# RWKV-6 and a hardswish MLP on one core: more fill products in the idle time of TensorE

## The chip, the cores and the metric

One of the eight cores of a Trainium2 chip runs the whole program. The metric is the device time of one execution in microseconds (us); "before" has a median of 565.46 us over five timed runs.

## The reference

An attention block in the manner of RWKV-6 on r, k, v, w of shape (4 batches, 8 heads, 768 steps, 48), float32, and then an MLP. The recurrence keeps a 48x48 state per batch and head:

```
for t in range(S):
    cur = u * k[t] (outer) v[t]
    y[t] = r[t] @ (state + cur)
    state = w[t][:, None] * state + k[t] (outer) v[t]
x = y transposed to (3072, 384)
h = x @ w_in                        # 384 x 2048
out = (h * clip(h + 3, 0, 6) / 6) @ w_out   # 2048 x 384
```

All products on TensorE are in float32. The weights arrive as 64-bit floats and are converted to float32 on the chip.

## The kernel before, in words

The 3072 tokens are 24 chunks of 128; four chunks make a block, so there are six blocks of the MLP. Per chunk the recurrence is done in closed form: two scans on VectorE give decays (L420, L429), r and k are scaled with them (L444, L440), TensorE makes the 64x64 scores (L488), transposes k (L504), makes the state product k'v (L588), reads the state (L566) and adds the scores' part (L575). The bonus u enters as a diagonal: r*k on VectorE (L453), a dot with u on TensorE (L463, called "the dot" below), a copy to ScalarE's side (L469), and eight scaled identities (L479) into the score tile, into which L495 copies the scores.

In block 0 the heads' last pair is read first (L566, L575), left by ScalarE (L630 or L632), spread with a selecting product (L640), then the rest is read (L566, L575) and left (L650, L652). As soon as chunks 0 and 1 are left, the first MLP products of block 0 follow: up (L695), clip on ScalarE (L685), gate on VectorE (L706). The weights' conversion goes on beside this: fetch (L379, by SP), ScalarE L388 and L392, VectorE L397, L402, L407. Three fetched tiles ("bits") at a time are held; the next fetch waits until L402 and L388 are done with an old one. L509 turns out the transposed k, L595 the state product, L517 and L533 update the state.

Nothing of the order is left to the hardware or a scheduler at run time: class `Plan` holds every step with its engine, an assumed duration, its predecessors, a due time and the buffers that it takes. `order()` plays the steps through with the assumed durations and gives one static order per engine; each engine then runs its list in order and waits at semaphores.

`emit()` writes the program out in that order. On the way it also writes fill products: `spin()` is a 128x128x128 float32 product of the identity with itself into a PSUM bank that is free at that time, and nobody reads it. Where the plan has TensorE idle between two steps, `int(FILL * hole / SPIN)` fill products go ahead of the second step; this lasts until the step "up0.0.0", the first up product of block 0, ahead of which none is put. `last` starts at `COLD` = 3.0, the planned time up to which the start is covered by four fill products that are written out by hand in `constants()`. The planned holes come from the assumed durations, not from the chip. A fill product stands in TensorE's queue as any other: what follows it on TensorE waits until it has been issued.

In the profile a float32 product shows as two records (a transpose as one).

## Time and profile before

| what | value |
|---|---|
| timed runs, five | median 565.46 us, 563.54 to 567.07 |
| profiled execution: time, span | 562.15 us, 560.2 us |
| TensorE (PE) busy | 541.9 us (97%) |
| VectorE (DVE) busy | 444.6 us (79%) |
| ScalarE (ACT) busy | 266.2 us (48%) |
| GpSimd (POOL) busy | 113.7 us (20%) |
| granted TensorE clock, mean | 0.986 |
| fill products (L1232), all before 23.6 us | 62 records, 31 products |
| first up product (L695) starts | 33.44 us |

The span runs from the first instruction to the last. PEclk in the strips is the clock granted to TensorE, in tenths of full speed; in tables of stretches it is a share. A name such as "PE ps L463" is engine, written tile, line. "idle before <- X" is the time in which the engine stood still ahead of an instruction, and what ended it.

### The profile page before, as it was taken

To read this page: it belongs to the slowest core of one execution; us is meant where nothing else is said; L and a number is where in the kernel's file an instruction comes from. 1 tells how busy PE (TensorE), PEld (TensorE's weight loads), DVE (VectorE), ACT (ScalarE), POOL (GpSimd) and SP (SyncE) were. 2 spreads that over 40 slices of the span, in tenths; PEclk is the share of its full clock that TensorE was granted. 3 is DMA by queue.
4 is the path that set the end of the run, shared out by engine and by line. 5 is a ranking of instruction groups with operands and counts; after the bars stand their busy time and mean duration, and the time that the engine had idled before them with its cause. 6 is when DMAs were issued, how large, how long until landed. Compare 5 with 4: busy or idle time off the path is not lost.

```text
span 560.2 us, 13278 instructions
## 1 busy us (share of the span) xinstructions
PE 541.9 (97%) x5512; PEld 482.7 (86%) x5512; DVE 444.6 (79%) x727; ACT 266.2 (48%) x657; POOL 113.7 (20%) x111
## 2 busy tenths in 40 slices
PE   7899999999899999999999999999999999999996
PEld 7788776778788899888899888899888899988995
DVE  6979999999979968789978789978797817087440
ACT  4677883653366524456524456524465720255100
POOL 2000000334263333145133144243321000000000
PEclk9879999999999999999999999999999999999999
DMA  8939823441342414765214765314500000100001
GB/s 258 277 125 330 279 96 102 133 139 29 115 153 81 102 56 157 237 193 156 95 57 157 235 197 151 100 56 157 185 16 0 10 8 15 43 1 1 1 15 48
DMA packets 23077, 63.96 MB, mean 114 GB/s; under 512 B 3120, under 2 KB 10352, under 8 KB 23008
## 3 DMA queue, kind: packets, MB, share of 16 engines
q1 hardware_dynamic: 22880, 63.02, 36.7%
q8 instruction: 45, 0.74, 0.6%
q14 instruction: 24, 0.20, 0.1%
q10 hardware_dynamic: 128, 0.00, 0.0%
HBM read 57.31 MB, written 4.72 MB: 111 GB/s over the span
## 4 chain that ended last, share of the span: by engine, by line
PE 66%; DVE 23%; DMA 4%; issue 2%; ACT 2%; SPq 1%; DVEq 0%; ACTq 0%
PE bank L866 24%; PE bank L809 23%; PE bankS L866 5%; PE bankS L809 4%; PE bank L695 3%; DMA bits<-in_moe_w_out_dram 2%; DVE E L420 2%; DVE g L826 2%; DVE W L429 2%; PE y_ps L566 1%; DMA xT<-xT 1%; PE y_ps L588 1%; PE ps L504 1%; PE bank L488 1%; DVE A L495 1%
## 5 line engine op out<-in xcount | busy, mean ns | idle before, releaser
L830 ACT ACTIVATE clip<-g,three 128x512 f32<-128x512 f32 x80 | 56.6, 719 | 43.6 <-DVE g L826 32.2
L826 DVE TENSOR_TENSOR g<-bank,g 128x512 f32<-128x512 f32 x80 | 53.7, 682 | 19.2 <-PE bank L809 19.0
L866 PE MATMUL bank<-w_out,g 128*128 128x192 f32 x352 | 63.3, 327 | 0.0
L834 DVE SCALAR_TENSOR_TENSOR g<-clip,g 128x512 f32<-128x512 f32 x80 | 57.8, 734 | 6.0 <-ACT clip L830 6.0
L866 PEld LDWEIGHTS bank<-w_out,g 128*128 128x128 f32 x352 | 58.0, 190 | 0.7
L440 POOL TENSOR_TENSOR K<-feat_in,E 112x512 f32<-112x512 f32 x17 | 21.9, 1290 | 152.1 <-DVE W L444 96.3
L479 ACT ACTIVATE A<-eyes,dg 128x64 f32<-128x64 f32 x192 | 49.0, 337 | 4.5 <-DVE dg L471 3.6
L882 ACT ACTIVATE o<-bank 128x192 f32<-128x192 f32 x33 | 10.9, 331 | 77.3 <-PE bank L866 77.3
L695 PE MATMUL bank<-xT,w_in 128*128 128x256 f32 x192 | 46.6, 393 | 1.0 <-DVE g L706 1.0
L695 PEld LDWEIGHTS bank<-xT,w_in 128*128 128x128 f32 x192 | 36.6, 196 | 7.4 <-DVE g L706 1.9
L662 ACT COPY xT<-y_ps 48x256 f32<-48x256 f32 x80 | 29.3, 366 | 28.8 <-PE y_ps L575 26.9
L809 PE MATMUL bank<-xT,w_in 128*128 128x256 f32 x160 | 41.4, 381 | 0.0
L824 ACT COPY g<-bank 128x512 f32<-128x512 f32 x50 | 28.9, 580 | 17.5 <-PE bank L809 17.3
L444 POOL TENSOR_TENSOR W<-feat_in,W 112x512 f32<-112x512 f32 x17 | 22.0, 1294 | 66.7 <-DVE W L429 66.7
L809 PEld LDWEIGHTS bank<-xT,w_in 128*128 128x128 f32 x160 | 29.9, 190 | 4.4 <-DVE g L826 0.4
L420 DVE TENSOR_TENSOR_SCAN E<-feat_in,back 112x520 f32<-112x520 f32 x24 | 30.4, 1269 | 2.7 <-POOL K L440 1.6
L809 PE MATMUL bank<-xT,bits 128*128 128x256 f32 x120 | 31.1, 381 | 0.0
L866 PE MATMUL bank<-more,g 128*128 128x192 f32 x176 | 30.5, 327 | 0.5 <-DVE o L884 0.5
L866 PE MATMUL bankS<-w_out,g 128*128 128x192 f32 x176 | 30.9, 327 | 0.0
L429 DVE TENSOR_TENSOR_SCAN W<-feat_in,start 112x520 f32<-112x520 f32 x24 | 29.8, 1245 | 1.1 <-PE y_ps L566 0.7
L866 PEld LDWEIGHTS bank<-more,g 128*128 128x128 f32 x176 | 28.6, 190 | 0.8 <-DVE o L884 0.8
L866 PEld LDWEIGHTS bankS<-w_out,g 128*128 128x128 f32 x176 | 28.7, 190 | 0.1
(285 smaller groups left out, 1160.7 us busy)
## 6 DMA issues: line engine op xcount, KB each, us to landing
feat_in<-in_feat_dram SPq DMA_DIRECT2D x23, 675.9 KB, 6.0
bits<-in_moe_w_in_dram SPq DMA_DIRECT2D x8, 768.0 KB, 9.1
bits<-in_moe_w_out_dram SPq DMA_DIRECT2D x8, 768.0 KB, 5.2
feat_in<-in_moe_w_in_dram SPq DMA_DIRECT2D x8, 768.0 KB, 4.4
feat_in<-in_moe_w_out_dram SPq DMA_DIRECT2D x8, 768.0 KB, 4.3
rk_in<-in_tok_dram SPq DMA_DIRECT2D x15, 384.0 KB, 6.0
v_in<-in_tok_dram SPq DMA_DIRECT2D x24, 192.0 KB, 4.2
out_dram<-o SPq DMA_DIRECT2D x24, 192.0 KB, 2.4
```

Source lines behind the costliest of these rows:

```text
L420: nc.vector.tensor_tensor_scan(out=E_[:, ::-1], data0=d["w"][:, :0:-1], data1=back.rearrange("q p t -> q (p t)")[:, ::-1], initial=0.0, op ...
L429: nc.vector.tensor_tensor_scan(out=W_, data0=d["w"][:, :-1], data1=starts[i % 2].rearrange("q p t -> q (p t)"), initial=0.0, op0=ALU.mult, ...
L444: early(i).tensor_mul(d["R"], d["r"], d["R"])
L479: nc.scalar.activation(out=d["A"][:, h, :], in_=eyes, func=ACT.Copy, scale=d["dg"][:, h])
L662: nc.scalar.copy(out=blocks[bk]["xT"][g * GP:g * GP + D, :, at:at + HL], in_=st[i]["y_ps"][a][(g ^ a) * GP:(g ^ a) * GP + D, :, :])
L695: nc.tensor.matmul(h_ps[:, :(c1 - c0) * L], lhsT=w_in[:, f // 2, j, f % 2, :], rhs=b["xT"][:, j, c0 * L:c1 * L], start=(j == 0), stop=(j = ...
L809: nc.tensor.matmul(b["p", d, c][:, z * HB:(z + 1) * HB], lhsT=weight(W_PLACE[r])[:, 2 * z + d, :], rhs=x_at(bk, X_PLACE[r]), start=fresh a ...
L824: nc.scalar.copy(out=out_, in_=src)
L826: nc.vector.tensor_tensor(out=out_, in0=src, in1=out_of(bk, d, other), op=ALU.add if sign > 0 else ALU.subtract)
L830: nc.scalar.activation(out=c, in_=out_of(bk, d, u), func=ACT.Relu, bias=three, scale=1.0)
L834: nc.vector.scalar_tensor_tensor(out=g, in0=blocks[bk]["r", d, u], scalar=6.0, in1=g, op0=ALU.min, op1=ALU.mult)
L866: nc.tensor.matmul(b["d", p, to][:, :h], lhsT=a, rhs=w(), start=(f == 0 and k in (1, 5)), stop=(f == HF - 1 and k in (2, 3, 4)), skip_grou ...
```

## The change

Two constants of the plan change. `FILL` goes from 0.75 to 1.0: a planned hole is filled wholly instead of three quarters. `SPIN`, the time that a fill product is reckoned to take, goes from 0.28 to 0.25 us: more of them are reckoned into the same hole. Both are used only in `emit()`, for the number of fill products; the plan's own order of steps does not depend on them.

```
-    SPIN = 0.28
-    FILL = 0.75
+    SPIN = 0.25
+    FILL = 1.0
     COLD = 3.0
     spin = until = None
```

## The prediction

> **What bounds the kernel now.** I read the strip of 40 slices first, for the TensorE clock.

> ```profile
> span 560.2 us, 13278 instructions
> ...
> PEclk9879999999999999999999999999999999999999
> ```

> The clock is below full only in the first three slices, 0 to 42 us, and that is where every fill product stands. The table of one-us stretches gives a clock of 0.96 in 15 to 16, 0.83 in 19 to 20, 0.58 in 26 to 27, 0.80 in 36 to 37, 0.50 between the first two and between the last two, and 1.00 elsewhere from 1 to 45. At half speed for the missing share, the clock fell at 15.92, rose at 19.33, fell at 26.16 and rose at 36.40. The distances are 3.41, 6.83 and 10.24 us: one, two and three steps of 3.41. So it is decided on a grid of that step, and I cut the table of stretches on the grid (columns: stretch, PE busy, PEld, DVE, ACT, POOL, clock, DMA share, GB/s).

> ```profile
> 9.09:12.51 3.42, 2.74 (x50) 2.56 (x51) 2.15 (x4) 2.12 (x10) 0.00 (x0) 1.00 1.05 360
> 12.51:15.92 3.41, 2.21 (x59) 1.77 (x49) 3.41 (x7) 2.90 (x11) 0.00 (x0) 1.00 1.08 373
> 15.92:19.33 3.41, 3.32 (x24) 2.74 (x24) 3.24 (x8) 3.34 (x6) 0.00 (x0) 0.50 1.05 210
> ...
> 22.75:26.16 3.41, 1.83 (x22) 1.37 (x22) 3.24 (x6) 1.96 (x8) 0.00 (x0) 1.00 1.02 292
> 26.16:29.57 3.41, 3.41 (x18) 3.41 (x18) 3.07 (x5) 2.19 (x10) 0.00 (x0) 0.50 1.05 382
> 29.57:32.99 3.42, 3.30 (x44) 2.83 (x44) 3.18 (x5) 1.84 (x5) 0.00 (x0) 0.50 0.36 130
> 32.99:36.40 3.41, 3.41 (x10) 2.87 (x11) 1.37 (x3) 2.23 (x11) 0.00 (x0) 0.50 0.00 0
> ...
> 67.12:70.53 3.41, 2.90 (x64) 2.41 (x62) 3.25 (x5) 2.89 (x4) 0.00 (x0) 1.00 0.99 339
> ```

> A stretch with PE busy 2.21 or 1.83 is followed by half clock; 2.74 and 2.90 keep it full. But 3.41 and 3.30 did not raise it again, and 3.32 did, so busy time is not the whole measure. I weigh each matmul record by its moving columns and by the share of the 128x128 array that it uses; transposes are left out. A fill record (128 columns, whole array) then counts 0.107 us. That gives 1.13 for the stretch at 9.09, 0.87 at 12.51, 0.65 at 22.75 and 0.98 at 67.12; at half clock, counted at full speed, 1.17 at 15.92 and 0.56 at 26.16. One mark between 0.87 and 0.98 explains all six. This measure is my inference.

> The chain of waits (start, us, what) shows what the second fall costs.

> ```profile
> 25.80 1.51 PE ps L463 x8
> 27.31 2.66 PE bank L640 x12
> 29.97 0.81 PE bank L566 x12
> ...
> 30.89 0.89 PE bank L575 x24
> 31.79 1.79 PE ps L463 x8
> 33.58 14.51 PE bank L695 x60
> ```

> From 25.80 on the chain is TensorE, nearly all of it at half clock. In the timeline VectorE pays for it (start, us, operation, idle before):

> ```profile
> 10.30 0.69 DVE L453 TENSOR_TENSOR rk<-feat_in 112x512 f32<-112x512 f32 x1 [2.03 <-DMA feat_in<-in_feat_dram]
> ...
> 33.80 0.56 DVE L397 TENSOR_SCALAR top<-bits 128x768 int32<-128x768 int32 x1
> 36.90 0.42 DVE L706 SCALAR_TENSOR_TENSOR g<-clip,bank 128x256 f32<-128x256 f32 x1 [2.54 <-ACT clip L685]
> ```

> It idles 2.54 us before the first gate (L706). The weight conversions stand behind that gate in its queue, SP's next fetch waits for the conversion L402 that ends at 38.18, and the DMA share is 0.00 from 33 to 39. So that idle time delays everything after it. The first fall costs nothing: from 10.30 to 25.6 VectorE has no wait over 0.14 us, and the chain lies on it.

> The fill products in the PE timeline, two records to a product:

> ```profile
> 1.43 5.63 PE L1232 MATMUL bankS<-ident 128*128 128x128 f32 x30 [1.43 <-POOL ident masks.py:199]
> ...
> 22.63 0.94 PE L1232 MATMUL bankS<-ident 128*128 128x128 f32 x6
> 24.71 0.32 PE L566 MATMUL bank<-W,S 48*48 48x64 f32 x4 [1.14 <-DVE S L517]
> ```

> **The change, part by part.** A planned hole of 1 us got 0.75/0.28 = 2.7 products and gets 1/0.25 = 4. In the built programs the holes go 15, 0, 4, 1, 4, 4, 3, 0 to 21, 1, 6, 2, 6, 6, 5, 1: 31 products to 48. Nothing else moves: the other engines' instructions and SP's queue keep their order. In the timeline 8 records started 0.11 us apart (the row of 1.07 us at 9.38, its last record 0.275 long), so a product takes 0.22 us at full clock; at half clock the 12 records of L640 in 2.80 us give 0.21 a record, 0.43 a product. So 17 x 0.22 = 3.8 us of TensorE work are added at full clock.

> *Before the first dot (+6).* The last 12 records run at full clock: +1.34 us. The fill now ends about 8.2, where L463 started at 7.12, so the first dot is 1.2 late. Behind it on PE wait the scores, the transposes, the second dot and the state product; on ACT, L469, the eight copies L479 (2.02) and L509. VectorE's next step waits for a DMA until 10.30 anyway, and the late dot has ended by 9.4. Followed along ACT: L469 at 9.3, copies to 11.6, L509 to 12.0; second dot 12.1 to 13.2, L469 13.2, copies 13.4 to 15.4, L509 to 15.8, L595 to 16.2. VectorE needs L595 at 16.55 (L517); before it ended at 15.92. Cost nothing; the cover left is 0.3 us.

> *The holes to 19.7 (+1, +2, +1, +2, +2).* The 1.2 us hole at 13.2 closes, since the second dot and the state product now fall into it, and the stretch at 12.51 gets several tenths more work: 0.87 rises well over 0.98. The clock should stay full at 15.92, so that six products take 1.3 us where four took 1.7. They end no later. Nothing won or lost: VectorE holds the chain.

> *The hole at 22.6 (+2).* Four more records lie ahead of a wait for VectorE (1.14 us, L517), so they cost nothing in time. They add 0.43 to the 0.65 of the stretch: 1.08, above the mark. By busy time alone it is 1.83 + 0.45 = 2.28, between 2.21 (fell) and 2.74 (kept). I take the first measure, since it alone also explains the rises.

> *Before L640 (+1).* This one lies on the path: 0.22 at full clock, 0.43 at half.

> **What it gives if the clock holds at 26.16.** From 25.80: dot 0.9, product 0.22 (the copies L630 end at 26.12, no wait), L640 1.34, L566 0.5, L575 with its drain and end 0.7, so about 29.5; the copies L650 and L652 take 0.97, during which the next dot runs; L695 from 30.6, its first six records 1.3 and an end of 0.16: 32.0, where it was 36.36. TensorE is 4.4 us earlier. VectorE cannot use all of that: its row L397 ends at 34.36, and of its own waits since 24.3 the 0.30 for L463 goes, so the gate comes at 34.0 for 36.90. ACT fits: copies to 33.4, clip (0.48) to 33.9. Gain 2.9. If the clock falls at 29.57 all the same, L695 ends its six records at 30.6 + 2.8 = 33.4, still ahead of VectorE, but the second gate, six records later at half clock, comes at about 36.5 for 38.28: gain 1.8. Late next are VectorE and the DMAs behind it, which keep the gain. I take 2.5. By the profiled execution's own time that is 562.15 - 2.5 = 559.65. That execution lay 3.3 under the median of the timed runs, 565.46; the difference is carried over: 565.46 - 2.5 = 563.0. Ends: 1.8 and the whole 4.4, so 561.1 to 563.7.

> [...]

> **Rivals.** *The clock falls at 26.16 all the same* (busy time decides; or the grid lies so that the thin stretch from 23.4 to 27.2 fills one step). Then TensorE is 0.43 later from L640 on, and the rise at 36.40 gives part back: +0.3, 565.8. For it: 2.28 is nearer to 2.21, and 0.8 us of idle remains. Against: the single mark.

> *The fill holds up the first dot for longer than its cover* (slower). The grid is tied to nothing in the trace that the kernel does, and the timed runs spread over 3.5 us. If the first rise came one step later, at 9.09, 42 records would end at about 9.9 and the first dot start 2.8 late; 30 end by 8.1, 1.0 late, which the cover takes. L595 would then end at about 17.95 and VectorE be 1.45 late; with 0.43 before L640 that is +1.9: 567.3. It decides once the first dot is later than about 8.5. Against: in this profile it is 8.2.

> *The change does nothing*: excluded for the counts, which differ; for the time it is the first rival.

> **How the numbers follow.** The clock holds: 0.55. It falls all the same: 0.27. The dot is late: 0.18. A measurement of this kernel tells 0.3% (1.7 us) from no change; the three lie at -2.5, +0.3 and +1.9, so faster 0.55, same 0.27, slower 0.18. The range reaches from the whole head start, 561.0, to the slower rival, 567.3; the likeliest case alone is 561.1 to 563.7.

> **What would show it.** Right: no half clock between 19 and 36 in the slices, L640 in about 1.45 us instead of 2.80, L695 starting near 31, the idle before the first L706 under 0.3 us, fetches starting again near 35, and L595 ending by 16.5. Wrong: L640 still 2.8 us long (first rival), or L517 after 16.9 with ACT named as what it waited for (slower rival).

## The result, and the profile after

The changed kernel takes as long as the one before: median 565.12 us (561.7 to 568.9, 52 runs) against 564.31 us (94 runs), ratio 1.0008, 95% interval 0.9996 to 1.0019. Ratios leave out single executions over 1.5% above the fastest of their kernel. The forecast was 563.0, reckoned from the 565.46 of five runs; from 564.31 the same gain would have been 561.8. The time lies in the range given, but that range spans the two rivals as well, and the case called likeliest did not occur: TensorE's clock still falls in the middle of block 0's first part. The profiled execution of after took 567.1 us, with a mean clock of 0.982.

The page of after, its span and the clock in 40 slices:

```profile
span 565.0 us, 13346 instructions
...
PEclk9979979999999999999999999999999999999999
```

The third slice (28 to 42 us) is below full as it was before, and slice 6 (70 to 85) is new. The second slice, low before, is full. Stretches of one us place the events: full from 5.93, half from 26.41 to 36.65 and from 70.79 to 77.61. The distances are again steps of 3.41 us. The table of stretches of after, cut on that grid (columns as in the prediction):

```profile
9.35:12.76 3.41, 3.41 (x56) 3.08 (x55) 2.77 (x4) 2.70 (x11) 0.00 (x0) 1.00 1.05 388
12.76:16.17 3.41, 3.41 (x83) 3.13 (x83) 3.41 (x8) 2.95 (x12) 0.00 (x0) 1.00 1.10 356
...
23.00:26.41 3.41, 2.26 (x28) 1.80 (x26) 3.27 (x5) 1.37 (x7) 0.00 (x0) 1.00 1.04 366
26.41:29.83 3.42, 3.42 (x23) 3.30 (x24) 3.28 (x6) 3.08 (x11) 0.00 (x0) 0.50 0.82 300
...
67.37:70.79 3.42, 2.90 (x66) 2.54 (x65) 3.39 (x5) 2.56 (x4) 0.00 (x0) 1.00 1.01 352
```

TensorE is busy without a gap from 9.35 to 16.17, and the fall that before had at 15.92 is gone. The stretch that ends at 26.41 holds 2.26 us of busy time where 2.28 was worked out, but by the prediction's weights its work is 0.66, where 1.08 was foreseen; before it was 0.65. The timeline of TensorE shows why (its first line is the first dot, 1.24 us later than before, where 1.2 was reckoned):

```profile
8.36 0.95 PE L463 MATMUL ps<-u_col,rk 112*128 112x2 f32 x8
...
22.29 1.38 PE L1232 MATMUL bankS<-ident 128*128 128x128 f32 x10
24.38 0.32 PE L566 MATMUL bank<-W,S 48*48 48x64 f32 x4 [0.71 <-DVE S L517]
...
26.88 2.66 PE L640 MATMUL bank<-xT,S__115 112*128 112x64 f32 x12
```

The ten fill records begin at 22.29, and the step that decides begins at 23.00: six of them start in the step ahead. What remains until 26.41 is small products, with few columns or little of the array in use. L640 takes 2.66 us, as before (2.80). VectorE, and the chain of waits of after (start, us, what), are therefore where they were:

```profile
36.47 0.42 DVE L706 SCALAR_TENSOR_TENSOR g<-clip,bank 128x256 f32<-128x256 f32 x1 [2.86 <-ACT clip L685]
```

```profile
25.47 1.02 PE ps L463 x8
26.49 0.59 PE bankS L1232 x2
27.09 2.45 PE bank L640 x12
```

The gate waits 2.86 us where it waited 2.54, and the added product before L640 is now a piece of the chain, 0.59 us at half clock, where 0.43 was reckoned. The fall at 70.79 holds up a gate as well; before has this gate at 75.80, without a wait:

```profile
77.50 0.42 DVE L706 SCALAR_TENSOR_TENSOR g<-clip,bank 128x256 f32<-128x256 f32 x1 [1.70 <-ACT clip L685]
```

### The profile page after: what moved, and what is told of

The parts are those of the page before. It is cut to its first block, busy times and chain, and to the rows that moved or that the text cites. A ratio compares the mean times of both kernels' runs of the same rounds, so it can differ in the third digit from the quotient of the medians.

```text
span 565.0 us, 13346 instructions
## 1 busy us (share of the span) xinstructions
PE 547.8 (97%) x5546; PEld 487.5 (86%) x5546; DVE 446.8 (79%) x727; ACT 265.9 (47%) x657; POOL 111.2 (20%) x111
## 4 chain that ended last, share of the span: by engine, by line
PE 68%; DVE 23%; DMA 3%; issue 2%; ACT 1%; SPq 0%; DVEq 0%
PE bank L866 24%; PE bank L809 21%; PE bank L695 6%; PE bankS L866 5%; PE bankS L809 4%; DVE g L826 2%; DMA xT<-xT 2%; DVE W L429 1%; DVE g L834 1%; DVE E L420 1%; DMA feat_in<-in_feat_dram 1%; PE y_ps L588 1%; PE y_ps L566 1%; DVE top L402 1%; DVE A L495 1%
## 5 line engine op out<-in xcount | busy, mean ns | idle before, releaser
L826 DVE TENSOR_TENSOR g<-bank,g 128x512 f32<-128x512 f32 x80 | 53.7, 682 | 18.1 <-PE bank L809 17.9
L479 ACT ACTIVATE A<-eyes,dg 128x64 f32<-128x64 f32 x192 | 49.0, 336 | 4.5 <-DVE dg L471 3.6
L695 PE MATMUL bank<-xT,w_in 128*128 128x256 f32 x192 | 48.5, 405 | 1.0 <-DVE g L706 1.0
L695 PEld LDWEIGHTS bank<-xT,w_in 128*128 128x128 f32 x192 | 38.2, 204 | 8.2 <-DVE g L706 1.7
L809 PE MATMUL bank<-xT,w_in 128*128 128x256 f32 x160 | 41.5, 382 | 0.6 <-DVE g L826 0.6
L809 PEld LDWEIGHTS bank<-xT,w_in 128*128 128x128 f32 x160 | 29.8, 190 | 5.5 <-DVE g L826 1.6
```

The lines of the kernel that those rows point to most:

```text
L479: nc.scalar.activation(out=d["A"][:, h, :], in_=eyes, func=ACT.Copy, scale=d["dg"][:, h])
L695: nc.tensor.matmul(h_ps[:, :(c1 - c0) * L], lhsT=w_in[:, f // 2, j, f % 2, :], rhs=b["xT"][:, j, c0 * L:c1 * L], start=(j == 0), stop=(j = ...
L809: nc.tensor.matmul(b["p", d, c][:, z * HB:(z + 1) * HB], lhsT=weight(W_PLACE[r])[:, 2 * z + d, :], rhs=x_at(bk, X_PLACE[r]), start=fresh a ...
L826: nc.vector.tensor_tensor(out=out_, in0=src, in1=out_of(bk, d, other), op=ALU.add if sign > 0 else ALU.subtract)
```

## The experiments

Two theories went in. *Theory one*: the clock falls between 22 and 31 us in nearly every execution, because the stretch with little weighted work is longer than one step; whatever the grid's phase, one whole step fits into it. I slid a window of 3.41 us over the trace: in before every window that starts from 22.4 to 31.8 weighs under 0.95, in after every one from 22.8 to 31.4; the thin stretch at 10 to 13 is gone in after. From 26 us on both traces run at half clock, which thins the windows by itself, so the slide alone does not show that the stretch would be as long at full clock. The profiles show that the fall is regular: all nine of kernels with fill of full width and without the nine products of held, below, have half clock somewhere between 22 and 36 us. *Theory two*: the clock is partly held, and the later first dot gives the gain back. Half-clock times below are 2 x span x (1 - mean clock), as the clock reads 1.00 or 0.50 in the profiles; they do not count the time before the first rise, where the tables have 1.00 though fill records start 0.21 us apart, for 0.11 behind it (before and after), and they count a fall at the very end (0.6 to 3.3 us in the profiles). By that every execution of after had 10.1 to 26.1 us of half clock, two steps or more, and 16.5 in the mean; where in an execution they lay, only its profile could tell.

Where no other edit is shown, a version only changes how many products stand ahead of a named step:

```
-    COLD = 3.0
+    COLD, MORE = 3.0, {...}
...
-   range(int(self.FILL * (self.start[n] - last) / self.SPIN) if n != self.until else 0)
+   range(int(self.FILL * (self.start[n] - last) / self.SPIN) + self.MORE.get(n, 0) if n != self.until else 0)
```

**held.** After, with `MORE = {'first1': 3, 'dot2': 2, 'read1': 1, 'dot3': 3}`: products through the whole thin stretch.

> The changed kernel with nine more fill products where the profile of after still shows thin work on TensorE: 3 before the first read of chunk 1 (8 instead of 5), 2 before the third dot (there were none), 1 before L640 (2 instead of 1), 3 before the fourth dot (there were none). Theory T1 (the clock falls between 22 and 27 us in nearly every execution, because the thin stretch is longer than one step of 3.41 and the change adds little in it): the clock now stays full from its first rise past 37 us, L640 takes about 1.45 us, the first gate L706 comes near 34 instead of 36.5, and the time falls by 2 to 3 us against before, 0.996. Theory T2 (the change holds the clock in part of the executions and the late first dot gives the gain back): half of that at most, about 1 us, since the dot is as late as in after.

Measured: 562.48 us median, ratio 0.9992 [0.9964, 1.002]; half clock 7.0 us in the mean. In its profile the clock is full from 5.92 to 558.9 us, L640 takes 1.45 us, and L695 starts at 31.45 (33.01 in after). So nine products in the right place hold the clock in this execution, and TensorE's price in the prediction (L640 in 1.45 us, L695 near 31) is met. Not in all: seven of the twelve executions have a mean clock of 0.994 or over and take 561.8 us in the mean, the other five, at 0.985 to 0.992, take 564.5. The gain over before can't be told from none here.

**narrow.** After, with fill products of 2 moving columns. It leaves out 126 of the 128 columns of each fill product.

```
-nc.tensor.matmul(still[:, at:at + L], lhsT=ident, rhs=ident, ...
+nc.tensor.matmul(still[:, at:at + 2], lhsT=ident, rhs=ident[:, :2], ...
```

> The changed kernel with every fill product 2 columns wide instead of 128; the weight load, the count and the places stay. If the clock goes by moving columns and array share (the measure of the prediction): the clock does not rise before the up products, that is not before 35 us, and the time is 2 to 6 us over before. If it goes by TensorE being busy: the clock falls and rises as in after, within 1 us of it.

Measured: 577.69 us, ratio 1.026 [1.0209, 1.031]. The timeline of TensorE in narrow:

```profile
1.43 9.12 PE L1232 MATMUL bankS<-ident 128*128 128x2 f32 x42 [1.43 <-POOL ident masks.py:199]
...
39.40 2.80 PE L640 MATMUL bank<-xT,S__115 112*128 112x64 f32 x12
```

TensorE is occupied for 9.12 us without a break, and still runs at half clock 30 us later (L640 2.80); the first rise comes at 48.74, 3.07 us after the full-array products L695 start (45.67). So busy time alone did not raise the clock here; the moving columns of the fill, 2 for 128, are what parts this kernel from after, whose clock rose at 5.93. This is the disputed measure tried by itself, and busy time is out; the share of the array was not varied by itself.

**nofill.** After with `FILL = 0.0`.

> The changed kernel with FILL = 0: the four products written out by hand alone. T1: no rise before the up products, everything on TensorE up to about 36 us at half clock; the time lies 2 to 6 us over before, close to the kernel with narrow products. T2: the same, but a part is given back since the first dot starts at once, 1 to 4 us.

Measured: 567.89 us, ratio 1.0088 [1.0055, 1.0121]; first rise at 38.29, 2.94 us after L695 starts (35.35). Against no fill from the plan at all, the fill of before is worth some 5 us (3.1 to 6.8 by the interval).

**firstfall.** Before, with `MORE = {'score0': 1, 'dot1': 2, 'turn1': 1, 'first0': 2, 'read0': 2}`: only the products that take away the first fall.

> The kernel before with eight of the change's products alone: those in the five holes after the first dot up to 19.7 us, so that only the first fall of the clock (15.92 in the profile of before) goes. T1: it goes in the profile, and the time stays within 0.2% of before, since VectorE holds the chain there. Rival: the first fall costs something too, and the time falls by 0.3% or more.

Measured: 563.07 us, ratio 0.9992 [0.9965, 1.0019]. Half clock in the mean 15.5 us, against 18.9 in the runs of before on the same chip: a step's worth less, and no time for it. The profile is full from 4.90 to 25.38 and half from there to 39.03. "The first fall costs nothing" holds, to within the interval of 1.5 us either way.

**again.** The kernel before, once more, for how its own executions differ.

> The kernel before, unchanged, for the clock of each of its executions. T1: no execution keeps the clock full between 22 and 36 us, so the mean clock of every one is at 0.991 or less (10 us at half clock are 0.009 of the span) and their mean near 0.985, as in the executions of the changed kernel; its profile shows L640 at 2.6 us or more again. T2: the falls come and go, so executions near 0.995 and near 0.98 stand side by side, and the time goes with the clock.

Measured: 564.15 us, ratio 1.0017 [0.9987, 1.0047]. Its profile has half clock without a break from 13.79 to 41.09, where the first one had two falls of one and three steps. The mean clocks run from 0.971 to 0.986: none of its executions is without half clock.

**start21 and start30.** Before with `MORE = {'dot0': 6}` (21 products ahead of the first dot), and after with `MORE = {'dot0': 9}` (30).

> The kernel before with six more products ahead of the first dot alone (21 for 15). T1: a first dot later than about 8.6 us delays VectorE one for one (in the run with 30 it was 4.0 late and VectorE 2.45 late), so an execution whose clock rises late pays up to 1 us and the mean is 0.2 to 0.4 us over before, 1.0005. T2: the six products cost about 1.3 us, 1.0023, which after wins back elsewhere.

> The changed kernel with 30 fill products instead of 21 before the first dot: the suspected cost of the late dot is more than doubled. T1: the first dot starts near 10.4 instead of 8.4, L595 ends near 18 and the gates of VectorE follow, so about 1.3 us slower than after, 1.003 against before; that after's own 21 are covered is then a matter of the place where it begins. T2: after already pays for its six, so the nine here cost the full 2.0 us, 1.004 or more.

Measured: start21 565.21 us, 1.0023 [0.9998, 1.0048]; start30 567.3 us, 1.0062 [1.0035, 1.0089]. In start30's profile the first dot comes at 11.12, and L533 on VectorE at 19.38 for 16.94 before: a dot 4.0 us later makes VectorE 2.44 late, so 1.56 is covered and the cover ends at a dot of 7.12 + 1.56 = 8.7. The prediction had 8.5. The mechanism of the slower rival is real; with six products it is small. In start21's profile L517 waits for it:

```profile
16.35 0.36 DVE L517 TENSOR_TENSOR S<-kvs,w_min 112x192 f32<-112x192 f32 x1 [0.15 <-ACT kvs L595]
```

There L517 comes 6.88 us after the second chunk starts on VectorE (L453, at 9.47), where it comes 6.25 us after it in before (10.30). It is 6.30 in after (L453 at 9.92) and 6.26 in held (10.39), both with 21 products. So by these profiles the six products cost 0 to 0.6 us at L517, more the earlier that chunk comes in.

**held2.** After with `MORE = {'dot0': -6, 'first1': 3, 'dot2': 2, 'read1': 1, 'dot3': 3, 'dot4': 4}`, the last four behind the first up product (`emit()` also lets a named step have products there): the short start, and cover for the thin stretch near 67 too.

> The kernel with the clock held, made cheaper and longer: the first dot gets 15 products as before instead of 21, and four products go ahead of the fifth dot at 68 us, where the clock fell in the profile of after at 70.8. T1: the clock stays full from the first rise to the end in nearly every execution (mean clock 0.994 or more), the first L706 comes near 34, and the time is 0.995 to 0.998 of before. If the lead is given back behind the small DMAs at the edges of the blocks, the profile still shows 2.5 us of lead at 220 us and less at the end, and the ratio is 0.998 to 1.000.

Measured: 563.42 us, ratio 0.999 [0.9954, 1.0027]; half clock 6.8 us in the mean. Its profile is full from 7.28 to 403.22, but its executions spread from 559.1 to 570.8, and the time goes with the clock: six take 559.1 to 562.5 at 0.994 and over, six 564.4 to 570.8 at 0.992 and under, and where the clock falls in those is not on record. In its profile VectorE is 3.3 us ahead of before's at 230 us and level at the end, as the last case of the expectation has it. The fall at 403 takes 1.6 of that, and the rest is not clearly the lead itself: VectorE in after, which has no lead, loses some 2 us against the same profile of before over that stretch. It decides nothing by itself.

**after_again, undo6, no640, held_start15.** Run together on one chip: after as it is; after with `MORE = {'dot0': -6}`; with `{'read1': -1}`; and held with `'dot0': -6` added.

> The changed kernel as it is, as the mark for the next three on the same chip. Both theories: 1.0008 of before, within 0.9985 to 1.003; half clock from about 26 to 37 us in its profile.

> The changed kernel with the six added products ahead of the first dot taken back (15 there, as before); the other eleven stay. Theory one (all that matters is the fall between 22 and 27 us, which stays, and the six products are covered): the same time as the changed kernel, within 0.4 us. Theory two (the shorter half clock of the changed kernel is worth some 1.7 us and the later first dot gives it back): 1.0 to 1.5 us under the changed kernel, 0.998 to 0.9985 of before. Both: the half clock still begins near 26 us.

> The changed kernel without the one product ahead of the spread product L640. The prediction's price for that product is 0.22 us at full clock and 0.43 at half: 0.2 to 0.4 us under the changed kernel. A price of 1 us or more would make it the thing that takes the gain back.

> The changed kernel with 3, 2, 1 and 3 products more ahead of the later steps to L695, so that the clock holds, and with the six products ahead of the first dot taken back. Theory one: as the version with the same late products and the long start, 0.9992 of before (562.5 us). Theory two: a further 1.0 to 1.5 us under that, 0.9965 to 0.9975 of before, about 561.5 us. Both: full clock from the first rise to the end of block 0's first part.

Measured, with before at 563.8 us in the same runs:

| kernel | median us | ratio to before, 95% | half clock, mean us |
|---|---|---|---|
| after_again | 565.76 | 1.0035 [1.0016, 1.0053] | 17.9 |
| undo6 | 564.05 | 1.0008 [0.9983, 1.0034] | 14.5 |
| no640 | 564.56 | 1.0009 [0.9994, 1.0023] | 16.1 |
| held_start15 | 561.91 | 0.9958 [0.9942, 0.9974] | 3.1 |

The last version beats both kernels: 0.42% under before, 2.4 us by the ratio (1.5 to 3.3 by its interval, which does not reach zero). All its nine executions have a mean clock of 0.994 or over; held2, with the same fill up to the first up product, has six of twelve, so that it holds always is not shown. Its page, TensorE's timeline and VectorE's first gate:

```profile
span 560.4 us, 13358 instructions
...
PEclk9999989999999999999999999999999999999999
```

```profile
22.20 2.05 PE L1232 MATMUL bankS<-ident 128*128 128x128 f32 x16
...
25.47 0.71 PE L1232 MATMUL bankS<-ident 128*128 128x128 f32 x4
...
26.83 0.69 PE L1232 MATMUL bankS<-ident 128*128 128x128 f32 x4
27.36 1.45 PE L640 MATMUL bank<-xT,S__115 112*128 112x64 f32 x12
```

```profile
34.24 0.42 DVE L706 SCALAR_TENSOR_TENSOR g<-clip,bank 128x256 f32<-128x256 f32 x1 [0.22 <-ACT clip L685]
```

The products stand on both sides of the waits at 24 and 26 us, L640 takes 1.45 us, and the gate waits 0.22 us, for 2.54 before. This is the profile that the prediction described under "Right". Held has the same row of the gate, figure for figure. Counted from the second chunk's start on VectorE, which moves with the DMA, the first gate comes after 26.60 us in before, 26.55 in after, and 23.85 in held, held2 and held_start15: the held clock gives 2.7 us there, with 15 products ahead of the first dot or with 21. In undo6, where the clock falls only at 27.56 and so behind L640 (1.45 us), it comes after 25.10:

```profile
34.46 0.42 DVE L706 SCALAR_TENSOR_TENSOR g<-clip,bank 128x256 f32<-128x256 f32 x1 [1.47 <-ACT clip L685]
```

In again, with half clock from 13.79 on, it comes after 29.57. So where in the thin stretch the half clock begins sets what it costs.

What the six products ahead of the first dot cost can be taken from three pairs: start21 against before, +0.23% (half width of the interval 0.25); after_again against undo6, +0.27% (0.31, from both intervals); held against held_start15, +0.34% (0.32; different chips, each against its own before). Weighted by the widths that is 0.27% with 0.17 either way, 1.5 us with 0.9. Three things speak against so much: the 52 runs of after gave 1.0008, no more than undo6; in two of the pairs the longer start also had more half clock (17.9 against 14.5 us, 7.0 against 3.1), which may be part of the difference; and the profiles show 0 to 0.6 us at L517 and none at the first gate of held. That they cost something in some executions is shown by start21's L517; 1.5 us is not shown. For the one product before L640 the difference to after_again is 0.26% (0.24), against a predicted 0.2 to 0.4 us (0.04 to 0.07%); with after at 1.0008 it would be nothing. Its price stays open between those, and leans on the same twelve executions of after_again. Theory one holds for the fall. Of theory two the late dot's price is left, its size open: half-clock time went, but by firstfall of a kind that cost nothing, so there was no gain to give back.

## Why the prediction was right and wrong, step by step

**The clock and its measure** (first part). Right in what it chose, too sharp in its mark. The 3.41 us grid stands in every profile that has a fall: half clock lasts one and three of its steps in before (15.92 to 19.33, 26.16 to 36.40), three and two in after, four in firstfall, eight in again. The 0.107 us of a fill record is half of the 0.213 that parts the starts of two at half clock in before. That busy time alone did not raise the clock, and that the moving columns count, is shown by narrow (9.12 us busy from 1.43 on, first rise at 48.74); that the array's share counts was assumed. A pair of steps says the same; the stretch tables of after_again:

```profile
24.99:28.40 3.41, 2.85 (x32) 2.51 (x32) 3.34 (x7) 1.85 (x10) 0.00 (x0) 1.00 1.04 378
28.40:31.81 3.41, 3.29 (x45) 2.82 (x44) 3.17 (x5) 2.72 (x10) 0.00 (x0) 0.50 0.40 144
```

Busy for 2.85 us the clock fell, by the weights at 0.76; in before it held with 2.74, at 1.13. But "one mark between 0.87 and 0.98 explains all six" was six points only. Ten profiles have falls in their first 120 us, 17 in all. With each record counted in the step in which it starts, 12 come after steps of up to 0.90 and five after steps of 1.07 to 1.39. Of 268 steps there after which the clock stayed full, one lies under 0.94 (0.86) and eight between 0.98 and 1.20. The measure sorts most steps, with a band of overlap: it does not account for all of them.

**The holes to 19.7.** Right for the first profile of after, which lost the fall at 15.92, and in the price (firstfall: nothing won). In after_again a fall at 14.74 is left, behind a step with TensorE busy for 2.66 us, probably since the thin steps there depend on when the dots come; VectorE then waits once for TensorE:

```profile
16.37 0.78 DVE L495 COPY_PREDICATED A<-mask,bank 128x256 f32<-128x256 uint8 x2 [0.33 <-PE bank L488]
```

**The hole at 22.6 (+2).** This is the step that failed, and it turned the forecast. Its sum, 0.65 + 0.43 = 1.08, assumed that the fill stands in the step that decides. It counted the grid of one execution as fixed, though the same text says in its second rival that the grid is tied to nothing. The fill began 0.3 us earlier in after's profile, the step 0.25 later, and 0.66 came out. And it is hardly bad luck with one edge: the windows that are too thin start from 22.8 to 31.4 us in after's trace, so filling the first part of the stretch only moves the fall. Its profile and those of after_again, undo6, no640 and start30, with the same fill in this hole, all have one between 25 and 32 us, and no execution of after has a mean clock over 0.991. Where the fall came behind L640, as in undo6, part of the gain was there. The first rival named the phase ("the grid lies so that the thin stretch from 23.4 to 27.2 fills one step") and got 0.27; by the sliding window it should have had most of the chance. Its time, 565.8, is 0.7 above the median of after. That 565.12 lies in the forecast's range is owed to that rival, not to the sum.

**What a held clock gives.** Right where it could be tried: 2.5 us foreseen (1.8 to 4.4), 2.7 in the profiles at the first gate and 2.4 measured in held_start15, which has the short start. With the 21 products of the forecast's own case (held) the times give 0.5 us, with 1.6 either way. "VectorE and the DMAs behind it … keep the gain" holds by the time of held_start15.

**Before the first dot (+6).** The mechanism and the point from which it decides were right (8.5 foreseen, 8.7 from start30). "Cost nothing; the cover left is 0.3 us" was mis-sized: it took one execution for all. In after's own profile L595 ends at 16.19, as reckoned (16.2), and L517 starts at 16.22: the DMA landed 0.38 us earlier than in before, and the cover was gone. In the profiles with fill of full width the first chunk after the DMA starts on VectorE (L453), where nothing but the DMA holds it, between 9.02 (again) and 10.39 (held and held_start15), and TensorE's first rise lies between 4.50 and 7.51; a cover of 0.3 us does not outlast that. The three pairs put the price at 1.5 us with 0.9 either way, the profiles at 0 to 0.6; the six products are all that parts held from held_start15, and yet VectorE's rows in the two agree to 0.01 us from L453 at 10.39 to the first gate. A first rise as late as the 9.09 of the slower rival was in none of these profiles.

**The third fall**, at 70.79 in after, was not foreseen: the step at 67 weighed 0.98 in before and was read as safe; in after it weighs 0.89. It has a price: at the gate of 77.50 VectorE falls 1.7 us behind before, and it is 2.0 behind at 129 us, of the 5 us by which after's profiled execution is slower. It comes and goes (a step in held_start15 from 69.84, none in undo6), and start21, which is before with six products, has it too (74.47), so it is a thin place of both kernels; whether the change makes it likelier is not shown.

In sum: the change takes away half-clock time that cost nothing in firstfall (1.5 us either way), leaves the fall that costs, and may pay a little for it at the first dot and before L640.

## What to carry to other kernels

Where a clock is decided on a free grid, as here on one of 3.41 us with a first rise between 4.50 and 7.51, ask for the weighted work of every window of one step's length that can lie in the stretch, not for the steps of the one profile: by the measure used here, 12 of the 13 steps of up to 0.90 were followed by a fall, so a stretch in which such a window is left was not safe here. Place fill by where VectorE holds the chain, on both sides of its waits, and keep it short ahead of the first work whose lateness is passed on; here 15 products there and nine more later (held_start15, 561.91 us) beat a plan that fills every hole (after_again, 565.76). And a cover of a few tenths of a us, read from one execution, was no cover here, where the work behind a DMA's landing (L453) starts anywhere from 9.02 to 10.39.

## What the hardware showed that was not expected

The fill of narrow kept TensorE occupied for 9.12 us from 1.43 on, over two and a half such steps, and the clock rose at 48.74. TensorE was as occupied by products that move two columns as by those that move 128: 9.12 us for 42 records, against 7.09 us for the same number of full ones in after, 4.5 of them at half clock. Yet the clock rose no sooner with the narrow fill than without: 3.07 us after L695 starts in narrow, 2.94 us after it in nofill.
